# Where the raw words of the last two weights land: idle halves of the weight ring in place of the attention tiles

## The chip, the cores and the metric

The kernel runs on one core of a Trainium2 chip. The metric is device microseconds of one execution; the kernel before takes 754.57 us (median of three runs, 754.39 to 755.67). The change is judged against that time. Engines: TensorE (PE in the profile; PEld is its weight load), VectorE (DVE), ScalarE (ACT), GpSimd (POOL) and SyncE (SP), whose queue issues every DMA here.

## The reference

Four batches of 576 positions, 8 heads of 64. Each batch goes through three parts, one after the other.

```python
# attention: full resolution in a band of 7 positions, plus 1/4 resolution over all
out = up(softmax(q_d k_d^T / 8) v_d) + softmax(mask(q k^T / 8)) v
# mixer: x is out as 576 x 512 per batch
u  = x + Re(FFT_seq(FFT_model(x)))
un = (u - mean(u)) / sqrt(var(u) + 1e-6)
x  = u + relu(un @ w_ch1) @ w_ch2          # 512 -> 2048 -> 512
# gated output
gate = sigmoid(causal 5-tap convolution of x with conv_w)
y = (gate * (x @ w_val)) @ w_out           # 512 -> 512 -> 512
```

The weights arrive as 64-bit numbers. The kernel reads them as pairs of 32-bit words and builds float32 from them itself.

## The kernel before, in words

Work is written as small steps with positions on one axis; the unit of that axis is a *unit*, 192 positions of a batch, and there are three to a batch (`units`, twelve in all, (0, 0) to (3, 2)). `spread` gives a list of steps positions between two numbers, all steps are sorted by position and issued, and a scheduler then reorders instructions on each engine by what it thinks is ready. So a change of positions can move any row after it. The first attention, the weights and unit 0 are start-up; from unit 1 on TensorE multiplies float16 pairs: each product is three matmuls (high by high, high by low, low by high).

**A unit.** `ln(b, j)` norms it: two column sums by TensorE (`st<-uc`, then `st<-sq`), a subtraction, a square on ScalarE, a reciprocal root of nine small VectorE steps (`vv`, `r`), and at the end the halves `uh` (ScalarE) and `ul` (VectorE). Then eight `h_group`s (24 matmuls into `ph`; ScalarE makes `hh`, VectorE `hl`) and eight `c_group`s (24 matmuls into `pc`) alternate; `c_group(g)` needs `hl` of group g. `fin` adds `pc` into X. Behind a unit come its taps (`tap`, and `W<-X,cw` later on), `val` (24 matmuls for each half) and `out`.

**Attention of the next batches** is mixed into the units. For batch 1: `scores` (dS) and its exponentials (dP, on ScalarE, one 64-column piece per instruction), `values` (dPT, PT, dO, and the copies `X<-dO`), then the 1/4-resolution part: `v` is pooled from four pieces of two tiles, each loaded by SP, added by GpSimd (`ptv`, `vr`), and then squared by ScalarE (`v<-v`), which frees the tile for a later load; `sc`, `E`, the multiply of E by `lsu` on GpSimd, `eT`, `ET`, `po`, `base`. After `base` come the transforms (FH, FL, `ab`, AH, AL, `pp`, `pq`, DS) that end in batch 1's X, and with it in `ln(1, 0)`.

**PSUM and X.** `dO`, `po`, `st`, `val` and `out` share two banks, so a matmul into `st` waits until an older `dO` has been copied by `X<-dO`.

**Weights.** `W[1]` to `W[20]` are 4 KB halves of ten ring tiles. `load_w` puts raw words of w_ch1 and w_ch2 into places that are not used yet; `word_w` makes float32 from them by three VectorE instructions for each 512 or 1024 columns (`to_f32`: one TENSOR_SCALAR, two SCALAR_TENSOR_TENSOR); `conv_w` splits float32 into high (ScalarE) and low (VectorE) float16. The splits of w_ch2 (W2 below; rows `W<-W,s_w`) run one behind the other on the two engines. W[17] to W[20] will hold w_val (16, 17) and w_out (18, 19). Before, each of their eight raw pieces (512 KB) is loaded into one of the two attention tiles `k` and `v` of the pool `qkv` and converted in the same step, so at most two are in flight and each load waits for a tile to come free.

**SP.** DMAs are issued in the order of SP's queue; a DMA that waits for its tile holds all behind it. `chain` makes early loads issue one after the other.

Of the kernel before, what the change touches and what calls it, by code (L numbers as in the profile page):

```python
# [12 lines left out]
I32 = mybir.dt.int32  # L13
# [4 lines left out]
B, H, S, D = 4, 8, 576, 64  # L18
# [31 lines left out]
S_S0 = (-11.1, -10.1)  # L50
# [3 lines left out]
S_END = -8.95  # L54
S_F0 = (-8.9, -8.1)
# [1 line left out]
S_N0 = -7.5  # L57
S_W2 = (-7.4, -6.9)
S_C2 = (0.89, 0.94)
S_W3 = (1.02, 1.6)  # L60
N_WARM = (8, 5, 14, 2, 2, 2)
S_G1 = (-6.8, -6.7)
S_G2 = (0.2, 0.44)
# [12 lines left out]
P_TAP = (-0.05, 0.35)  # L76
# [51 lines left out]
def attn_moe_kernel(ctx, tc, q_t, k_t, v_t, w1, w2, w_val, conv_t, w_out, c_feat, c_seq, c_band, c_eye, out):  # L128
    nc = tc.nc
    P = 128  # L130
    w1, w2, w_val, conv_t, w_out = (x.bitcast(I32) for x in (w1, w2, w_val, conv_t, w_out))

    def pool(name, bufs=1, **kw):
        return ctx.enter_context(tc.tile_pool(name=name, bufs=bufs, **kw))
# [29 lines left out]
    def stt(eng, out, in0, scalar, in1, op0, op1):  # L164
        return eng.scalar_tensor_tensor(out=out, in0=in0, scalar=scalar, in1=in1, op0=op0, op1=op1)  # L165
# [14 lines left out]
    chain = {"on": CHAIN, "last": None}  # L180

    def load(**kw):

        if chain["on"] and chain["last"] is not None:
            with tc.issue_after(chain["last"]):
                i = nc.sync.dma_start(**kw)
        else:
            i = nc.sync.dma_start(**kw)
        chain["last"] = i.ins
# [63 lines left out]
    NPOS = 20  # L253
    ring = [wp.tile([P, 2048], F32, name=f"W{2 * i + 1}") for i in range(NPOS // 2)]
    W = [wp.tile([P, 1024], F32, name="W0")]
# [11 lines left out]
    def rows(dst, src, c, c0, n):  # L267
        load(out=dst, in_=src[c * 128:(c + 1) * 128, 2 * c0:2 * (c0 + n)])
# [3 lines left out]
    def behind(gate, f):  # L272

        if gate is None:
            f()
        else:
            with tc.issue_after(gate):
                f()

    def to_f32(dst, raw, gate=lambda: None):  # L280

        r = raw.rearrange("p (n t) -> p n t", t=2)
        behind(gate(), lambda: V.tensor_scalar(out=dst, in0=r[:, :, 1], scalar1=3, scalar2=0x3FFFFFF8,
                                               op0=ALU.logical_shift_left, op1=ALU.bitwise_and))
        behind(gate(), lambda: stt(V, dst, r[:, :, 1], -0x40000000, dst, ALU.bitwise_and, ALU.bitwise_or))
        behind(gate(), lambda: stt(V, dst, r[:, :, 0], 29, dst, ALU.logical_shift_right, ALU.bitwise_or))
# [18 lines left out]
    def word_w(i):  # L305
        if i < 16:
            raw = raws.pop(i)
            n = 1024 // len(raw)
            for z, x in enumerate(raw):
                to_f32(W[i + 1].bitcast(I32)[:, z * n:(z + 1) * n], x,  # L310
                       lambda g=(gates, gates2)[i // 8]: g.pop(0) if len(g) > 1 else g[0])
            return
        assert "scored" in st[1]
        for a in range(2):
            raw = qkv.tile([P, 1024], I32, tag="kv"[a], name="raw")
            rows(raw, w_val if i < 18 else w_out, (i % 2) * 2 + a, 0, 512)
            to_f32(W[i + 1].bitcast(I32)[:, a * 512:(a + 1) * 512], raw)

    gram = {}

    def sumsq_w(i, key, first, last):

        if first:
            gram[key] = pst("cv", [P, P]) if key == "wo" else ps_c.tile([P, P], F32, tag="c1", name="gram")
        x = W[i + 1].bitcast(BF16).rearrange("p (n t) -> p n t", t=2)
        for c in range(8):
            blk = x[:, c * 128:(c + 1) * 128, 1]
            behind(st[0]["st2"].ins if i < 8 else None, lambda: T.matmul(
                out=gram[key], lhsT=blk, rhs=blk, start=(first and c == 0), stop=(last and c == 7)))
# [11 lines left out]
    def conv_w(i, s, eng):  # L341

        h_, l_, r_ = hi(i), lo(i), W[i + 1]
        A.activation(out=h_, in_=r_, func=AF.Copy, scale=s[:, 0:1])
        if eng is G:
            A.activation(out=r_, in_=r_, func=AF.Copy, scale=s[:, 0:1])
            G.tensor_tensor(out=l_, in0=r_, in1=h_, op=ALU.subtract)
        else:
            stt(eng, l_, r_, s[:, 0:1], h_, ALU.mult, ALU.subtract)
# [17 lines left out]
    def wv_scale():  # L367
        ps = pst("cv", [P, 512])
        for a in range(4):
            j = pr_t("sqv", [P, 512])  # L370
            A.activation(out=j, in_=W[17 + a // 2][:, (a % 2) * 512:(a % 2) * 512 + 512], func=AF.Square)
            T.matmul(out=ps, lhsT=ones, rhs=j, start=(a == 0), stop=(a == 3))
        mx = keep.tile([P, 1], F32, name="cvmx")
        V.tensor_reduce(out=mx, in_=ps, axis=AX.X, op=ALU.max)
        mx2 = keep.tile([P, 1], F32, name="cvmx2")
        V.tensor_scalar(out=mx2, in0=mx, scalar1=float(DM), scalar2=None, op0=ALU.mult)
        sc["sv"], sc["ivv"] = pow2(mx2, 14, "wv")

    def wo_scale():
        f = trace_w("wo")  # L380
        sc["so"], sc["ivo"] = pow2(f, 14, "wo")
        ivvo = keep.tile([P, 1], F32, name="ivvo")
        mul(V, ivvo, sc["ivv"], sc["ivo"])
        sc["ivvo"] = ivvo
# [3 lines left out]
    st = {}  # L388
# [524 lines left out]
    un = {}  # L913
    mainp = {}

    def main_pools():
        for n, bufs in (("un", 2), ("hg", 3), ("g", 1), ("L", 2), ("tap", 3), ("S", 3)):
            mainp[n] = pool("m_" + n, bufs)

    def l_t(name, shape):  # L920
# [281 lines left out]
    def w_in2(i):  # L1202
        if i >= 11:
            load_w(i)
        word_w(i)

    def w_in(i):
        word_w(i)
# [4 lines left out]
    def weights3_steps():  # L1213
        def first():
            to_f32(cw.rearrange("p a b -> p (a b)").bitcast(I32), craw)

        def a2():
            wv_scale()
            for i in range(16, 18):
                conv_w(i, sc["sv"], G if i in LO_G else V)  # L1220

        def a3():
            for i in range(18, NPOS):
                sumsq_w(i, "wo", i == 18, i == NPOS - 1)
            wo_scale()
            for i in range(18, NPOS):
                conv_w(i, sc["so"], G if i in LO_G else V)
        return [first] + [lambda i=i: word_w(i) for i in range(16, NPOS)] + [a2, a3]

    units = [(b, j) for b in range(B) for j in range(UPB)]  # L1230
    events = []
# [1 line left out]
    def put(pos, f):  # L1233
        events.append((pos, len(events), f))

    def spread(steps, p0, p1):
        tot = sum(c for c, _ in steps)
        acc = 0.0
        for c, f in steps:
            put(p0 + (p1 - p0) * acc / tot, f)  # L1240
            acc += c
# [16 lines left out]
    def close():  # L1258
        start.close()
        main_pools()  # L1260

    assert S_LD[1] <= S_T0[0] and S_L1 <= S_W1[0] and S_T0[1] <= S_S0[0] and S_S0[1] <= S_F0[0] and S_F0[1] <= S_N0
    assert S_W1[1] <= S_W2[0] and 8 / 17 < S_C1[0] and S_C1[1] <= S_C2[0] and 15 / 17 < S_C2[0]
    assert S_S0[1] <= S_END <= S_F0[0] and S_C2[1] <= min(S_W3[0], 1 + P_TAP[0])
    put(S_END, close)
    for b in range(1, B):
        steps = attn_steps(b)
# [7 lines left out]
        spread(steps[n1:], *P_E[b])  # L1275
        put(P_L[b], lambda b=b: urgent(lambda: ln(b, 0), "N"))
    w3 = weights3_steps()
    spread([(1.0, f) for f in w3], *S_W3)
    for n, (b, j) in enumerate(units):
        main = mlp_steps(b, j)  # L1280
        spread([(1.0, f) for f in main], n, n + 1)
# [63 lines left out]
```

## Time and profile before

| | |
|---|---|
| median of three runs | 754.57 us (754.39 to 755.67) |
| the profiled execution | 750.94 us, span 749.1 us |
| TensorE busy | 688.4 us (92%), granted clock 0.943 of full |
| VectorE busy | 482.2 us (64%) |
| ScalarE busy | 321.0 us (43%) |
| GpSimd busy | 108.2 us (14%) |

The profiled execution is 3.6 us below the median of the timed runs; 1.8 us of it lie outside the span. A wait is read from the engine that waits: the idle time ahead of a row stands in its brackets with what ended it. TensorE's clock of 1.00 is its full level (2.4 GHz), 0.50 the lower one (1.2 GHz).

### The profile page before, as it was taken

How to read it: one execution, taken by the hardware profiler on the slowest of the kernel's cores; microseconds unless marked ns; L12 is line 12 of the kernel's file. 1: busy time of each engine (PE TensorE's matmuls, PEld its weight loads, DVE VectorE, ACT ScalarE, POOL GpSimd, SP SyncE). 2: the span in 40 equal slices, each digit the busy share in tenths (PEclk: the TensorE clock that was granted, in tenths of full speed). 3: DMA queues.
4: the chain of work that ended last, by engine and by line, in shares of the span. 5: the costliest groups of instructions: out<-in, count | busy, mean ns of one | idle time of the engine just before them, and what ended most of it. 6: DMA issues, size and time to landing. Idle time of an engine off the chain costs nothing.

```text
span 749.1 us, 18445 instructions
## 1 busy us (share of the span) xinstructions
PE 688.4 (92%) x7811; PEld 599.7 (80%) x7811; DVE 482.2 (64%) x1073; ACT 321.0 (43%) x994; POOL 108.2 (14%) x143
## 2 busy tenths in 40 slices
PE   7877659987899998989999998899999999999996
PEld 3444449987788987877898997789989989999893
DVE  3795869768986967566976824747835473633334
ACT  2465211777644436665533645553423131322212
POOL 0400000004431012240203105103010010000000
PEclk8556779998999999999999999899999999999999
DMA  9955356123232110132140001002100000000001
GB/s 239 391 205 180 111 190 200 37 82 113 94 113 70 49 60 30 53 85 79 46 129 2 16 24 41 15 3 64 47 16 15 2 6 25 2 16 1 30 2 42
DMA packets 29005, 54.79 MB, mean 73 GB/s; under 512 B 2133, under 2 KB 17109, under 8 KB 27898
## 3 DMA queue, kind: packets, MB, share of 16 engines
q1 hardware_dynamic: 28922, 53.61, 21.9%
q8 instruction: 61, 1.00, 0.6%
q14 instruction: 22, 0.18, 0.1%
HBM read 46.52 MB, written 9.45 MB: 75 GB/s over the span
## 4 chain that ended last, share of the span: by engine, by line
PE 59%; DVE 22%; DMA 9%; ACT 6%; POOL 2%; issue 1%; SPq 1%; DVEq 0%; POOLq 0%; ACTq 0%
PE pc L1065 20%; PE ph L1047 19%; DVE W L165 8%; PE out L1152 5%; PE val L1136 5%; ACT dP L536 3%; DMA v<-in_v_dram 2%; PE po L716 2%; DVE tap L165 2%; PE ab L810 1%; DMA dr<-dx 1%; DMA dx<-X 1%; DMA X<-in_moe_w_ch_dram 1%; DMA raw<-in_moe_w_ch_dram 1%; DVE fF L787 1%
## 5 line engine op out<-in xcount | busy, mean ns | idle before, releaser
L1047 PE MATMUL ph<-uh,W 128*128 128x192 f16 x1408 | 197.4, 247 | 1.6 <-ACT uh L973 1.6
L1065 PE MATMUL pc<-hh,W 128*128 128x192 f16 x1408 | 196.1, 247 | 1.2 <-ACT hh L1051 1.2
L1065 PEld LDWEIGHTS <-W 128*128 128x128 f16 x2112 | 176.7, 98 | 14.4 <-issue 10.8
L1047 PEld LDWEIGHTS <-W 128*128 128x128 f16 x2112 | 176.6, 98 | 7.5 <-issue 5.2
L1065 PE MATMUL pc<-hl,W 128*128 128x192 f16 x704 | 172.7, 247 | 5.1 <-DVE hl L165 5.1
L1047 PE MATMUL ph<-ul,W 128*128 128x192 f16 x704 | 173.8, 247 | 0.0
L165 DVE SCALAR_TENSOR_TENSOR hl<-ph,hh 128x384 f16<-128x384 f32 x88 | 48.5, 553 | 92.3 <-ACT hh L1051 92.3
L1051 ACT ACTIVATE hh<-ph 128x384 f16<-128x384 f32 x88 | 43.3, 493 | 102.3 <-PE ph L1047 99.3
L165 DVE SCALAR_TENSOR_TENSOR W<-X,cw,W 128x192 f32<-128x192 f32 x160 | 61.0, 437 | 2.3 <-ACT W L1121 2.2
L1136 PE MATMUL val<-yy,W 128*128 128x192 f16 x576 | 53.3, 246 | 1.5 <-ACT osb L1164 1.1
L1136 PEld LDWEIGHTS <-W 128*128 128x128 f16 x576 | 47.9, 98 | 3.4 <-issue 1.9
L536 ACT ACTIVATE dP<-dS,dmx 128x64 f32<-128x64 f32 x160 | 47.9, 340 | 0.4
L1152 PE MATMUL out<-W,gh 128*128 128x512 f16 x144 | 45.9, 381 | 0.0
L536 ACT ACTIVATION_READ_ACCUMULATOR dP<-dS,dmx 128x1 f32 x160 | 37.2, 233 | 0.0
L1152 PE MATMUL out<-W,gl 128*128 128x512 f16 x72 | 27.5, 382 | 2.1 <-DVE gl L165 2.1
L165 DVE SCALAR_TENSOR_TENSOR W<-W,W 128x1024 int32<-128x1024 int32 x24 | 28.8, 1220 | 0.1
L682 ACT ACTIVATE E<-sc,nm 72x144 f32<-72x144 f32 x64 | 23.6, 374 | 6.6 <-PE po L716 6.4
L1152 PEld LDWEIGHTS <-gh 128*128 128x128 f16 x144 | 14.2, 99 | 14.4 <-issue 0.9
L1009 PE MATMUL ph<-u,W 128*128 128x192 f32 x128 | 24.3, 345 | 1.0 <-DVE u L945 1.0
L668 PE MATMUL sc<-qkT 64*72 64x144 f32 x128 | 22.4, 341 | 2.5 <-DVE qkT L588 1.0
L1143 ACT ACTIVATE gh<-W 128x384 f16<-128x384 f32 x20 | 10.6, 528 | 31.9 <-DVE W L165 31.8
L1121 ACT ACTIVATE W<-X,cw 128x192 f32<-128x192 f32 x40 | 15.5, 455 | 19.6 <-DVE X L165 17.8
(221 smaller groups left out, 1169.2 us busy)
## 6 DMA issues: line engine op xcount, KB each, us to landing
W<-in_moe_w_ch_dram SPq DMA_DIRECT2D x12, 1024.0 KB
v<-in_v_dram SPq DMA_DIRECT2D x32, 144.0 KB
out_dram<-osb SPq DMA_DIRECT2D x18, 256.0 KB
vw<-in_v_dram SPq DMA_DIRECT2D x16, 256.0 KB
X<-in_q_dram SPq DMA_DIRECT2D x6, 576.0 KB
kT<-in_k_dram SPq DMA_DIRECT2D x4, 582.0 KB
dx<-X SPq DMA_DIRECT2D x4, 576.0 KB
dr<-dx SPq DMA_DIRECT2D x4, 576.0 KB
```

The lines of the kernel that those rows point to most:

```text
L165: return eng.scalar_tensor_tensor(out=out, in0=in0, scalar=scalar, in1=in1, op0=op0, op1=op1)
L536: A.activation(out=s_[:, z, a], in_=pss[par][:, z, a], func=AF.Exp, scale=SCALE, bias=mx[:, par, z, a:a + 1], accum_out=su[:, par, z, a:a ...
L668: T.matmul(out=pss[par][:, qc], lhsT=d["qkT"][r, 0, a, qc * QC:(qc + 1) * QC], rhs=d["qkT"][r, 1, a, :], start=True, stop=True,)
L682: A.activation(out=E[:, qc], in_=ps[:, qc], func=AF.Exp, scale=SCALE / 16, bias=nm[:, qc:qc + 1], accum_out=su[:, qc:qc + 1],)
L716: T.matmul(out=po[par * 64:par * 64 + 64], lhsT=d["vr"][:, kc, (a % 2) * 4 + (a // 2) * 2 + par], rhs=ets[par][:, kc], start=(kc == 0), st ...
L1009: i = T.matmul(out=ps[:, e], lhsT=W[kc * 2 + m // 8 + 1][:, o:o + 128], rhs=u()[:, kc, :], start=(kc == 0), stop=(kc == 3))
L1047: T.matmul(out=ps[:, e], lhsT=w1_ap(pw, kc, 2 * g + e), rhs=uh[px][:, kc, :], start=(t == 0), stop=(t == 11))
L1051: A.activation(out=h_, in_=ps, func=AF.Relu)
L1065: T.matmul(out=ps[m // 2][:, m % 2], lhsT=w2_ap(pw, kk, m), rhs=x[px][:, e, :], start=(kk == 0 and (pw, px) == (0, 0) and m % 2 == 0), sto ...
L1121: A.activation(out=m, in_=x, func=AF.Copy, scale=w)
L1136: T.matmul(out=ps[:, e], lhsT=wv_ap(pw, kc, 2 * mh + e), rhs=m_["y"][px][:, kc, :], start=(t == 0), stop=(t == 11))
L1152: T.matmul(out=ps, lhsT=(gh, gl)[px][:, kc, t * 128:(t + 1) * 128], rhs=wo_ap(pw, kc), start=(n == 0), stop=(n == 11))
```

## The change

The raw words of w_val and w_out get other places, and loading is written apart from converting. The first two pieces of w_val go to W[19] and W[20], the third to a new 4 KB tile `rx`, the fourth to W[19] again once the first is converted; the first piece of w_out goes to W[20], the second to `rx`, and the last two to the attention tiles as before. Each of these loads is issued behind the last load of the chain. w_val's conversions stand at positions 0.945 to 0.99, just behind W2's splits (0.89 to 0.94), and w_out's at 1.0 to 1.5; before, all stood between 1.02 and 1.6.

```diff
--- before.py
+++ after.py
-S_W3 = (1.02, 1.6)
+S_W3 = ((0.945, 0.99), (1.0, 1.5))
...
-        assert "scored" in st[1]
         for a in range(2):
+            to_f32(W[i + 1].bitcast(I32)[:, a * 512:(a + 1) * 512], raw3.pop((i, a)))
+
+    raw3 = {}
+
+    def load_w3(i, a):
+
+        if (i, a) in ((16, 0), (17, 1)):
+            raw = W[19].bitcast(I32)
+        elif (i, a) in ((16, 1), (18, 0)):
+            raw = W[20].bitcast(I32)
+        elif i < 19:
+            raw = mainp["rx"].tile([P, 1024], I32, tag="rx", name="raw")
+        else:
+            assert "scored" in st[1]
             raw = qkv.tile([P, 1024], I32, tag="kv"[a], name="raw")
+        raw3[i, a] = raw
+        with tc.issue_after(chain["last"]):
             rows(raw, w_val if i < 18 else w_out, (i % 2) * 2 + a, 0, 512)
-            to_f32(W[i + 1].bitcast(I32)[:, a * 512:(a + 1) * 512], raw)
...
-        for n, bufs in (("un", 2), ("hg", 3), ("g", 1), ("L", 2), ("tap", 3), ("S", 3)):
+        for n, bufs in (("un", 2), ("hg", 3), ("g", 1), ("L", 2), ("tap", 3), ("S", 3), ("rx", 1)):
...
-        return [first] + [lambda i=i: word_w(i) for i in range(16, NPOS)] + [a2, a3]
+        ld = lambda *h: lambda: [load_w3(*x) for x in h]
+        return ([ld((16, 0), (16, 1), (17, 0)), first, lambda: word_w(16), ld((17, 1)), lambda: word_w(17)],
+                [ld((18, 0), (18, 1), (19, 0), (19, 1)), a2, lambda: word_w(18), lambda: word_w(19), a3])
...
-    spread([(1.0, f) for f in w3], *S_W3)
+    for g, p in zip(w3, S_W3):
+        spread([(1.0, f) for f in g], *p)
```

On SP, behind the q of batch 2 (`X<-in_q`), the queue was this; `v_...` are the tiles of batch 1's pooled v, `raw` the attention tiles:

```order
L188 DMA vw<-in_v_dram 64x2x256 x2
L188 DMA X<-in_q_dram 128x2x576 x2
L188 DMA raw<-in_moe_w_val_dram 128x1024 x2
L186 DMA v_1808<-in_v_dram 72x2x256
L188 DMA v_1850<-in_v_dram 72x2x256
L188 DMA v_1851<-in_v_dram 72x2x256
L188 DMA raw<-in_moe_w_val_dram 128x1024
L188 DMA v_1862<-in_v_dram 72x2x256
L188 DMA v_1863<-in_v_dram 72x2x256
L188 DMA raw<-in_moe_w_out_dram 128x1024
L188 DMA raw<-in_moe_w_val_dram 128x1024
```

and is now this (`W_121` is the ring tile of W[19] and W[20], `raw` the tile `rx`):

```order
L188 DMA vw<-in_v_dram 64x2x256 x2
L188 DMA X<-in_q_dram 128x2x576 x2
L186 DMA v_1811<-in_v_dram 72x2x256
L188 DMA v_1853<-in_v_dram 72x2x256
L188 DMA v_1854<-in_v_dram 72x2x256
L188 DMA v_1865<-in_v_dram 72x2x256
L188 DMA v_1866<-in_v_dram 72x2x256
L188 DMA W_121<-in_moe_w_val_dram 128x1024 x2
L188 DMA raw<-in_moe_w_val_dram 128x1024
L188 DMA W_121<-in_moe_w_val_dram 128x1024
L188 DMA W_121<-in_moe_w_out_dram 128x1024
```

The five loads of v now stand ahead of every load of w_val; before, two pieces stood ahead of the first and one among them.

On VectorE, from the split of W2 that follows the adds of unit 0's `fin` to the first `hl` of unit 1 (`W_120<-raw` is a conversion of w_val, `W_...<-W_...,s_w` a split):

```order
L283 TENSOR_SCALAR W_120<-raw 128x512
L165 SCALAR_TENSOR_TENSOR W_117<-W_118,s_w_1528,W_117 128x1024
L165 SCALAR_TENSOR_TENSOR tap<-X,cw,tap 128x192 x3
L165 SCALAR_TENSOR_TENSOR W_120<-raw,W_120 128x512
L165 SCALAR_TENSOR_TENSOR tap<-X,cw,tap 128x192 x4
L165 SCALAR_TENSOR_TENSOR W_120<-raw,W_120 128x512
L165 SCALAR_TENSOR_TENSOR tap<-X,cw,tap 128x192 x2
L945 TENSOR_TENSOR uc<-X,st 128x768
L165 SCALAR_TENSOR_TENSOR W_118<-W_118,s_w_1528 128x1024
L165 SCALAR_TENSOR_TENSOR tap<-X,cw,tap 128x192
L283 TENSOR_SCALAR W_120<-raw 128x512
L165 SCALAR_TENSOR_TENSOR hl<-ph,hh 128x384
```

and now:

```order
L165 SCALAR_TENSOR_TENSOR W_117<-W_118,s_w_1531,W_117 128x1024
L689 TENSOR_REDUCE nm<-sc 72x2 x2
L171 TENSOR_TENSOR X<-pc_1615,X 128x2x192
L165 SCALAR_TENSOR_TENSOR tap<-X,cw,tap 128x192 x2
L165 SCALAR_TENSOR_TENSOR W_118<-W_118,s_w_1531 128x1024
L165 SCALAR_TENSOR_TENSOR tap<-X,cw,tap 128x192 x9
L959 TENSOR_TENSOR uc<-X,st 128x768
L165 SCALAR_TENSOR_TENSOR tap<-X,cw,tap 128x192
L165 SCALAR_TENSOR_TENSOR W_118<-W_119,s_w_1531,W_118 128x1024
L165 SCALAR_TENSOR_TENSOR tap<-X,cw,tap 128x192
L165 SCALAR_TENSOR_TENSOR hl<-ph,hh 128x384
```

The conversions have left this piece (and three instructions of one that stood ahead of it); one more split and three more taps now stand ahead of `hl`.

On ScalarE, from the last `hh` of unit 2 to the `uh` of batch 1's unit 0 (`sq<-uc` is the square of `ln(1, 0)`, `dP` the exponentials of batch 2):

```order
L1051 ACTIVATE hh<-ph 128x384
L951 ACTIVATE sq<-uc 128x768
L528 ACTIVATE dmx<-dmx 128x8
L536 ACTIVATE dP_3073,dsu<-dS,dmx 128x64 x4
L536 ACTIVATE dP_3078,dsu<-dS,dmx 128x64 x4
L1164 ACTIVATE osb<-out,sof_3313 128x512
L1099 ACTIVATE yy<-X,s_y_2356 128x768
L973 ACTIVATE uh<-uc 128x768
L563 ACTIVATE PT<-dPT 128x512
L528 ACTIVATE dmx<-dmx 128x16
L536 ACTIVATE dP_3248,dsu<-dS,dmx 128x64 x8
```

and now:

```order
L1065 ACTIVATE hh<-ph 128x384
L542 ACTIVATE dmx<-dmx 128x8
L550 ACTIVATE dP_3072,dsu<-dS,dmx 128x64 x4
L550 ACTIVATE dP_3077,dsu<-dS,dmx 128x64 x4
L965 ACTIVATE sq<-uc 128x768
L542 ACTIVATE dmx<-dmx 128x16
L550 ACTIVATE dP_3247,dsu<-dS,dmx 128x64 x8
L1178 ACTIVATE osb<-out,sof_3312 128x512
L1113 ACTIVATE yy<-X,s_y_2441 128x768
L987 ACTIVATE uh<-uc 128x768
L550 ACTIVATE dP_3256,dsu<-dS,dmx 128x64 x8
```

The square now stands behind the first eight exponentials, and eight more stand between it and `uh`. On TensorE the two column sums of that norm moved with it: `st<-uc` stood 53 matmuls of unit 2 ahead of that unit's last one and now stands behind it, with two `dS<-bandb` and 32 `dS<-kT,X` between it and `st<-sq`.

## Rows read from the trace of the kernel before

**Rows 1.** Stretches: length, busy time of PE, PEld, DVE, ACT, POOL, clock, DMA share, GB/s.
```profile
173.00:192.00 19.00, 13.12 (x154) 11.25 (x153) 18.93 (x34) 15.52 (x40) 6.88 (x8) 0.82 0.36 122
...
300.00:330.00 30.00, 27.38 (x419) 24.06 (x420) 13.94 (x33) 21.41 (x82) 12.38 (x17) 1.00 0.27 77
...
330.00:460.00 130.00, 129.77 (x1655) 114.72 (x1653) 84.29 (x195) 64.05 (x213) 21.84 (x31) 1.00 0.14 47
```

**Rows 2.** TensorE's waits between 170 and 345 us: total, times, longest, in us.
```profile
PE st L939 <- ACT X L583: 4.3, 2, 4.0
...
PE pc L1065 <- DVE hl L165: 1.6, 1, 1.6
...
PE ph L1047 <- ACT uh L973: 1.6, 1, 1.6
...
PE st L939 <- POOL sq L171: 1.1, 1, 1.1
```

**Rows 3.** Timeline around 176 to 185 us: start, length, engine, line, operation, [idle before].
```profile
176.34 0.33 SPq L186 DMA_DIRECT2D v<-in_v_dram  x1
...
176.96 6.03 SPq L188 DMA_DIRECT2D v<-in_v_dram  x2
...
180.95 0.95 POOL L171 TENSOR_TENSOR vr<-v 72x256 f32<-72x256 f32 x1 [9.31 <-DMA v<-in_v_dram]
...
185.17 1.06 POOL L171 TENSOR_TENSOR vr<-v 72x256 f32<-72x256 f32 x1 [1.33 <-DMA v<-in_v_dram]
...
183.24 1.01 PE L939 MATMUL st<-uc,ones 128*128 128x192 f32 x2 [4.00 <-ACT X L583]
```

**Rows 4.** Conversions by tile (ns min/median/max), and the timeline around 190 us.
```profile
L165 DVE SCALAR_TENSOR_TENSOR W<-raw,W x24: 661/682/1211, 94.9 to 219.0; 128x512 int32<-128x512 int32 x24
...
L283 DVE TENSOR_SCALAR W<-raw x12: 408/424/947, 92.7 to 216.4; 128x512 int32<-128x512 int32 x12
...
188.04 1.27 DVE L165 SCALAR_TENSOR_TENSOR W<-W,s_w 128x1024 f16<-128x1024 f32 x1
...
190.90 0.74 DVE L165 SCALAR_TENSOR_TENSOR tap<-X,cw,tap 128x192 f32<-128x192 f32 x2
...
191.03 0.24 PE L1065 MATMUL pc<-hl,W 128*128 128x192 f16 x1 [1.60 <-DVE hl L165]
```

**Rows 5.** Timeline of GpSimd: its multiplies beside a full VectorE and alone.
```profile
195.94 5.65 POOL L168 TENSOR_TENSOR E<-E,lsu 72x288 f32<-72x288 f32 x2 [4.84 <-DVE lsu L687]
...
209.55 0.67 POOL L168 TENSOR_TENSOR E<-E,lsu 72x288 f32<-72x288 f32 x1 [0.55 <-DVE lsu L687]
```

**Rows 6.** Timeline from the last layer norm of batch 1, unit 0, to its first matmuls.
```profile
277.16 0.59 PE L939 MATMUL st<-uc,ones 128*128 128x192 f32 x2 [0.32 <-DVE uc L171]
...
279.01 0.83 ACT L951 ACTIVATE sq<-uc 128x768 f32<-128x768 f32 x1
...
279.88 0.95 DVE L171 TENSOR_TENSOR sq<-sq 128x384 f32<-128x384 f32 x2
...
282.33 0.52 PE L939 MATMUL st<-sq,ones 128*128 128x192 f32 x2
...
282.64 0.61 DVE L165 SCALAR_TENSOR_TENSOR X<-pc,iv,X 128x384 f32<-128x384 f32 x1
...
283.27 0.30 DVE L955 TENSOR_SCALAR vv<-st 128x192 f32<-128x192 f32 x1
...
288.63 0.84 ACT L973 ACTIVATE uh<-uc 128x768 f16<-128x768 f32 x1 [1.43 <-DVE uc L168]
...
289.45 1.28 DVE L525 TENSOR_REDUCE dmx<-dS 128x8 f32<-128x512 f32 x2
...
289.52 0.33 PE L1047 MATMUL ph<-uh,W 128*128 128x192 f16 x2 [1.60 <-ACT uh L973]
```

**Rows 7.** From the chain that ended last: start, length, engine, what.
```profile
163.17 2.38 ACT dP L536 x16
...
253.43 1.98 PE pc L1065 x24
```

More of the change, by code (lines that the diff above doesn't have):

```diff
@@ L1263, in attn_moe_kernel @@
     assert S_W1[1] <= S_W2[0] and 8 / 17 < S_C1[0] and S_C1[1] <= S_C2[0] and 15 / 17 < S_C2[0]
-    assert S_S0[1] <= S_END <= S_F0[0] and S_C2[1] <= min(S_W3[0], 1 + P_TAP[0])
+    assert S_S0[1] <= S_END <= S_F0[0] and S_C2[1] <= min(S_W3[1][0], 1 + P_TAP[0])
     put(S_END, close)
```

## The prediction

> **What bounds the kernel now.** I read the stretches first, for where TensorE stands still: a time in which it is dense can only be shortened by doing less, and the change takes no matmul away. From 330 to 460 us it is busy for 129.77 of 130 us [rows 1]; in 173 to 192 for 13.12 of 19 at a granted clock of 0.82, and in 300 to 330 for 27.38 of 30. The orders of the engines of the two kernels part only at about 173 us (where the first conversion leaves VectorE) and are the same again from about 445 us, so the result is the idle time of TensorE between these, plus what its clock does. Then the list of its waits, read for who ends them [rows 2]: `st` waited 4.0 us for the copy `X<-dO`, `pc` 1.6 for `hl`, `ph` 1.6 for the last `uh`, `st` 1.1 for a sum behind GpSimd. Last the timeline around each, for what the releaser itself was late with.
>
> The 4.0 us: ScalarE's `X<-dO` stands behind a square of `v`, that behind GpSimd's `vr` at 180.95, and that waited for a load of v issued at 176.34, which lay behind two raw pieces of w_val [rows 3]. `st` begins at 183.24, at half clock (1.01 us for a pair that takes 0.59 later [rows 6]). Of the chain that ended last, 24 matmuls cost 1.98 us and 8 exponentials with their read-outs 2.38 us [rows 7]; I use both as prices.
>
> **The change part by part.** *The load of v on SP* no longer has raw words ahead of it. The second load of v, with no raw piece in its way to the tile, was issued when the row of 176.96 ends, at about 182.7 (176.96 plus 6.03 is 182.99, its last descriptor 0.33), and its `vr` began at 185.17: 2.5 us, against 180.95 − 176.34 = 4.6 for the first [rows 3]. So 2.1 us are to be had on the load. But the new ScalarE order has one square of v more ahead of `X<-dO`, which wants one more load, issued only when its tile is free, and a tap and a split of W2. At one load and landing (2.5) plus the add (0.95) this takes the gain back. I take 0 for this wait; the bounds are −2.1, and +1.4 if the extra load also finds its tile late (2.5 + 0.95 − 2.1).
>
> *A, the first `hl` of unit 1.* In the piece of VectorE's order three TENSOR_SCALARs and four SCALAR_TENSOR_TENSORs of conversions are gone: 3 × 0.42 + 4 × 0.68 = 4.0 us [rows 4]. One split (1.27) and three taps (0.37 each) are new: 2.4. That is −1.6. VectorE is busy for 18.93 of 19 us there, so nearly all of it counts; but about 1.8 us of the removed work stood where the split and the adds wait for ScalarE, and if that wait stays, only 0.6 of the 1.6 is left. `pc` resumes at 191.03 now. I take −1.0, between −0.4 and −3.0 (the last if VectorE nowhere waits for ScalarE and the taps find their place in a gap).
>
> *B, the second sums of unit 1.* The conversions now stand behind that `hl`: split, three TENSOR_SCALARs, conversions, taps, 6.7 us at the prices above, before the adds that `st<-sq` needs. TensorE has 63 matmuls till there, 63 × 1.98/24 = 5.2 us, so it waits 1.5. Some conversions stood near these sums before as well, so part of that wait is there already; I take half, +0.7 (0 to +1.5).
>
> *C, the 1/4-resolution chain.* The conversions now lie beside GpSimd's multiplies of E. Beside a full VectorE two of these took 5.65 us, 2.8 each, against 0.67 alone [rows 5]; `eT` on TensorE waits for them. One multiply more in the full stretch would be +2.1 for that chain, most of it hidden by the h and c groups that TensorE takes in between. I take +0.4 (0 to +1.5). The Trainium skill ("SBUF — State Buffer", section "SBUF: two separate sides") has VectorE and GpSimd share a port pair which whoever starts first keeps for a whole instruction, the other blocked; by that C would be at its upper bound and the sum 1.1 higher. The rows of 2.8 against 0.67 agree that they hinder each other, and can't tell whether one instruction excludes the other fully.
>
> *D, the norm `ln(1, 0)` between unit 2 of batch 0 and the first unit of batch 1.* Call T the end of unit 2's last matmul: 282.33 before, since `st<-sq` follows at once [rows 6]. Before, `st<-uc` (277.16), ScalarE's `sq` (279.01) and its sums were all hidden under 53 matmuls, and `vv` began at T + 0.9, `uh` at T + 6.3. Now `st<-uc` stands behind T. The subtraction on VectorE (from 277.16 to 279.01 that step took 1.85) also stands behind the two `fin` adds (0.61 each), so `sq` starts at about T + 1.9, if the eight exponentials that now stand ahead of it (2.4) are done; 0.83 and the two adds of 0.95 bring T + 3.6; and the maxima `dmx` of the second group (1.28) have moved ahead of `vv`: T + 4.9. From `vv` to `uh` it is 5.36 us as before, and ScalarE's eight more exponentials, `osb` and `yy` (about 4 us) fit into that. `uh` is thus 4.0 us later after T (3.0 if the maxima run before the sums, 4.8 if the exponentials hold up `sq`). `st<-uc` with some of the `dS`, 0.6 us of matmuls, fills part of it. I take +3.4 of idle time, between +2.4 and +4.2, in pieces before `st<-sq`, `out` and `ph`.
>
> *E, given back.* The second group of exponentials and `dS` is no longer behind this `uh`, so the work of batch 2 that follows comes earlier by up to 2.4 us against TensorE. Of the 30 us from 300 to 330 it is idle for 2.6, 1.1 of them the `st<-sq` behind GpSimd [rows 1, 2]. If these go, that is −2.6; a first `hl` now stands behind 16 exponentials' sums on VectorE, +1.0. I take −1.6 (0 to −2.6, with no new wait). Behind 330 TensorE is dense and gives nothing back.
>
> *Without a price here.* That the loads land earlier, and that w_val's conversions end earlier, gains nothing by itself: TensorE's waits show none for w_val's tiles [rows 2]. The tile `rx` and the ring halves hold no one up; w_out's pieces follow later into tiles that are free.
>
> Sum: −1.0 + 0.7 + 0.4 + 3.4 − 1.6 = +1.9. Against the profiled 750.94 that makes 752.8; the runs' median lies 3.6 above the profiled execution, so I forecast 754.57 + 1.9, about 756.5 us.
>
> **The rivals.** *No change, 754.6.* D at its lower bound and A at −1.6, with B at 0 and C at 0.4, give −0.4. For it: most of what I move are waits of a microsecond, and a scheduler's order changes little where the slack is as large as VectorE's 64%. Against it: `st<-uc` can't run before T in the new order, whatever else happens. That the change doesn't do what it says (the landing places move and nothing waits for them) also ends here.
>
> *Faster, 752.4.* VectorE reaches the first `hl` by the sum of its own work, A −3.0, B 0, C 0, D +2.4, E −1.6: −2.2. It decides at the wait before `st` in the 180s: if `X<-dO` runs before the extra square of v, the 2.1 us of the load come on top of TensorE's front, and the clock isn't lowered there. For it: the raw words were in front of the load in the trace. Against it: the extra square in ScalarE's order.
>
> *Slower, about 759.4.* The idle pieces of D come close together, 5.0 us within 12 with the 1.6 that stood there, and TensorE drops to its lower level behind them, as it did after the 4.0 us wait at 183.24. That stretch had 0.82 of full clock over 19 us, 0.18 × 19 = 3.4 us, of which 2.9 fall on busy time; 756.5 + 2.9 = 759.4. Against it: the wait of 1.6 us at 289.52 is followed by full clock (two matmuls in 0.33). The Trainium skill ("TensorE: Matmul & The Clock Gate", section "HAM oscillation — how this bites in real kernels") describes kernels that pay a lower clock behind every long pause; the row at 183.24 agrees with it.
>
> **How the numbers follow.** Chances: the forecast (756.5, own range 755.0 to 758.0) 0.43, no change 0.27, faster 0.20, slower by the clock 0.10. About 1.5 us, 0.2%, is what a measurement of this kernel can tell from no change. The lower part of the forecast's own range is within that, the no-change case spreads beyond it on both sides: faster by over 0.2% 0.24, within 0.33, slower 0.43. Leaving out 2 in 10 at the ends I keep 751.8 (faster with the bound of the load, half of it) to 759.5 (the clock).
>
> **What would show it.** In the profile after: `st<-ACT X` at about 183 still near 4 us (the load gives nothing) or down to 2 (the faster rival). `pc<-DVE hl` at about 190. GpSimd's two multiplies of E near 196, longer than 5.65 or not. At the end of unit 2 of batch 0: `st<-uc` behind the last `pc`, `vv` at T + 4.9, `uh` at T + 10.3, and TensorE idle for 5 us and more between T and `ph`; a full clock there rules out the last rival. The wait `st<-POOL sq` near 329 gone. The prediction is wrong if the idle time from T to `ph` is not 2.4 to 4.2 us longer, or if the stretch before 262 us changes by more than the sum of A to C, 0.1, plus or minus 2.

## The result, and the profile after

The changed kernel takes 759.62 us (median of 6 runs, 757.3 to 761.08), before 754.18 in the same rounds: ratio 1.0069, 95% interval 1.0051 to 1.0087. By the ratio it is slower by 5.2 us, where 1.9 were forecast. The median lies 0.1 us above 759.5, the upper end of the forecast's range, and the six runs lie on both sides of that end. The profiled execution took 760.22 us, span 758.4.

Busy times by stretch of the kernel after (columns as in [rows 1]; the stretch from 192 to 210 us is new, and the second fence has it for the kernel before):

```profile
173.00:192.00 19.00, 12.04 (x146) 9.86 (x145) 16.93 (x27) 15.89 (x40) 6.45 (x8) 0.80 0.36 122
192.00:210.00 18.00, 15.71 (x144) 14.21 (x144) 15.61 (x42) 6.18 (x19) 7.76 (x3) 0.83 0.43 147
...
290.00:300.00 10.00, 6.84 (x83) 3.23 (x82) 8.04 (x18) 6.11 (x29) 3.08 (x4) 0.83 0.02 6
300.00:330.00 30.00, 29.39 (x503) 27.32 (x503) 15.63 (x35) 20.52 (x83) 9.43 (x11) 1.00 0.24 72
330.00:460.00 130.00, 127.52 (x1527) 111.51 (x1525) 87.40 (x201) 67.14 (x228) 23.24 (x32) 1.00 0.15 50
```

```profile
192.00:210.00 18.00, 17.00 (x197) 15.48 (x195) 17.38 (x48) 7.65 (x21) 7.91 (x5) 1.00 0.37 110
```

Two stretches have become worse. From 192 to 210 TensorE did 144 matmuls in place of 197, at a clock of 0.83 in place of 1.00. From 290 to 300 it was busy for 6.84 us, again at 0.83. The stretch from 300 to 330 lost its idle time, as forecast, but 2.5 us of idle time stand behind 330. A low clock in these stretches is no mark of the change by itself: a second profile of the order of before (`before_again`, at the end of the experiments) has the same two at 0.84 and 0.83:

```profile
192.00:210.00 18.00, 17.54 (x171) 16.20 (x172) 17.13 (x40) 10.64 (x30) 6.25 (x7) 0.84 0.32 106
290.00:300.00 10.00, 8.06 (x97) 7.03 (x88) 6.13 (x12) 7.72 (x39) 0.30 (x1) 0.83 0.08 28
```

TensorE's waits from 170 to 345 us, after (answers to [rows 2]):

```profile
PE st L953 <- ACT X L597: 3.7, 2, 3.5
PE pc L1079 <- DVE hl L165: 2.3, 1, 2.3
PE eT L720 <- POOL E L168: 2.3, 1, 2.3
PE dS L518 <- ACT dP L550: 2.0, 2, 1.2
PE sc L682 <- ACT E L696: 1.7, 2, 1.4
PE val L1150 <- ACT yy L1113: 1.4, 1, 1.4
...
PE st L953 <- DVE sq L171: 1.0, 1, 1.0
PE pc L1079 <- ACT hh L1065: 0.8, 1, 0.8
...
PE st L953 <- POOL sq L171: 0.2, 1, 0.2
```

The first place in the timeline, engine by engine (answers to [rows 3 to 5]):

```profile
179.90 0.80 POOL L171 TENSOR_TENSOR vr<-v 72x256 f32<-72x256 f32 x1 [7.75 <-DMA v<-in_v_dram]
...
184.14 0.75 PE L953 MATMUL st<-uc,ones 128*128 128x192 f32 x2 [3.48 <-ACT X L597]
...
183.74 4.55 DVE L165 SCALAR_TENSOR_TENSOR tap<-X,cw,tap 128x192 f32<-128x192 f32 x9
...
191.35 0.54 DVE L165 SCALAR_TENSOR_TENSOR hl<-ph,hh 128x384 f16<-128x384 f32 x1
...
191.94 0.32 PE L1079 MATMUL pc<-hl,W 128*128 128x192 f16 x1 [2.31 <-DVE hl L165]
...
195.59 6.44 POOL L168 TENSOR_TENSOR E<-E,lsu 72x288 f32<-72x288 f32 x2 [5.90 <-DVE lsu L701]
...
201.46 0.69 PE L720 MATMUL eT<-eye,E 72*72 72x72 f32 x4 [2.28 <-POOL E L168]
```

The load of v lands earlier (`vr` 3.0 us after its issue at 176.86, 4.6 before), and the wait before `st` is 0.5 us shorter. But nine taps at 0.51 us each, one behind the other, now stand ahead of `uc` and `hl` on VectorE, `hl` comes at 191.35, and GpSimd's two multiplies of E, 6.44 us beside the conversions, hold `eT` back by 2.28 us. The second place, `ln(1, 0)` (answers to [rows 6]):

```profile
288.12 0.52 PE L953 MATMUL st<-uc,ones 128*128 128x192 f32 x2
...
288.51 0.32 ACT L550 ACTIVATE dP<-dS,dmx 128x64 f32<-128x64 f32 x1
...
290.84 0.88 ACT L965 ACTIVATE sq<-uc 128x768 f32<-128x768 f32 x1
...
293.21 1.28 DVE L539 TENSOR_REDUCE dmx<-dS 128x8 f32<-128x512 f32 x2
294.41 0.34 DVE L969 TENSOR_SCALAR vv<-st 128x192 f32<-128x192 f32 x1
...
294.42 0.63 PE L1166 MATMUL out<-W,gl 128*128 128x512 f16 x1
...
297.68 0.38 PE L1166 MATMUL out<-W,gl 128*128 128x512 f16 x1
...
299.72 0.83 ACT L987 ACTIVATE uh<-uc 128x768 f16<-128x768 f32 x1
```

Unit 2 ends at T = 288.12. `vv` begins at T + 6.3 and `uh` at T + 11.6 (T + 0.9 and T + 6.3 before). The exponentials only start at 288.51, so ScalarE's `sq` stands behind them till 290.84, and the two sums behind it took 1.53 us beside a multiply on GpSimd (0.95 before). The matmuls into `out` take 0.63 us around 294 and 0.38 at 297.68: TensorE's clock was at its lower level there.

### The profile page after: what moved, and what is told of

It is laid out like the page before. It is cut to its first block, busy times and chain, and to the rows that moved or that the text cites. A ratio compares the mean times of both kernels' runs of the same rounds, so it can differ in the third digit from the quotient of the medians.

```text
span 758.4 us, 18452 instructions
## 1 busy us (share of the span) xinstructions
PE 694.4 (92%) x7811; PEld 601.8 (79%) x7811; DVE 485.5 (64%) x1073; ACT 321.5 (42%) x994; POOL 109.8 (14%) x143
## 4 chain that ended last, share of the span: by engine, by line
PE 58%; DVE 21%; DMA 11%; ACT 6%; POOL 2%; issue 1%; SPq 1%; DVEq 0%; ACTq 0%; POOLq 0%
PE pc L1079 19%; PE ph L1061 18%; DVE W L165 8%; PE out L1166 6%; PE val L1150 4%; DMA W<-in_moe_w_ch_dram 3%; ACT dP L550 2%; DMA v<-in_v_dram 2%; DVE tap L165 2%; PE po L730 1%; PE ab L824 1%; PE sc L682 1%; DMA dr<-dx 1%; DMA dx<-X 1%; DMA raw<-in_moe_w_ch_dram 1%
## 5 line engine op out<-in xcount | busy, mean ns | idle before, releaser
L1079 PE MATMUL pc<-hh,W 128*128 128x192 f16 x1408 | 198.3, 249 | 2.0 <-ACT hh L1065 2.0
L165 DVE SCALAR_TENSOR_TENSOR W<-W,W 128x1024 int32<-128x1024 int32 (+1 forms) x30 | 32.8, 1112 | 0.1
L730 PE MATMUL po<-ET,vr 72*64 72x144 f32 x128 | 20.2, 328 | 4.7 <-ACT ET L725 4.7
L1023 PEld LDWEIGHTS ph<-u,W 128*128 128x128 f32 x128 | 23.1, 208 | 1.6 <-DVE u L959 1.6
```

The costliest lines, as they stand in the source:

```text
L730: T.matmul(out=po[par * 64:par * 64 + 64], lhsT=d["vr"][:, kc, (a % 2) * 4 + (a // 2) * 2 + par], rhs=ets[par][:, kc], start=(kc == 0), st ...
L1023: i = T.matmul(out=ps[:, e], lhsT=W[kc * 2 + m // 8 + 1][:, o:o + 128], rhs=u()[:, kc, :], start=(kc == 0), stop=(kc == 3))
L1079: T.matmul(out=ps[m // 2][:, m % 2], lhsT=w2_ap(pw, kk, m), rhs=x[px][:, e, :], start=(kk == 0 and (pw, px) == (0, 0) and m % 2 == 0), sto ...
```

## The experiments

The table gives, for each kernel, the median of its timed runs, the ratio to before with its 95% interval, and from the profile the start of unit 0's `fin` (the first `X<-pc`) and the rest of the span behind it. The start-up ahead of `fin` differs by several us from one execution to the next, so profiles are compared by the rest. It is good to 2 or 3 us: the two profiles of the order of before differ by +0.8 in it, and by −1.6 if counted from an earlier matmul. `places` is the new landing places alone; `wout_old` is the change with w_out's group back at its old positions; `taps_behind` and `no_dO_wait` are the change with one more edit; `E_on_ACT`, `wout_old_no_dO_wait`, `both_moves` and `both_moves_E` start from `wout_old`; a name with `before_` is an edit of the kernel before. The kernels were timed in several rounds, in which the median of before lay between 753.9 and 754.7, so kernels of different rounds are compared by their ratios.

| kernel | median, us | ratio (95%) | `fin` at | rest |
|---|---|---|---|---|
| before | 754.18 | 1 | 177.40 | 571.7 |
| before_again | 755.03 | 1.0007 (0.9991 to 1.0022) | 179.39 | 572.5 |
| the change | 759.62 | 1.0069 (1.0051 to 1.0087) | 177.09 | 581.3 |
| places | 756.23 | 1.0036 (1.0015 to 1.0058) | 178.35 | 575.9 |
| wout_old | 756.46 | 1.0031 (1.0015 to 1.0047) | 178.41 | 575.9 |
| taps_behind | 768.88 | 1.0196 (1.0173 to 1.0219) | 178.38 | 589.0 |
| no_dO_wait | 754.27 | 1.0006 (0.9990 to 1.0022) | 178.05 | 573.5 |
| E_on_ACT | 753.73 | 1.0012 (0.9992 to 1.0031) | 178.20 | 573.2 |
| wout_old_no_dO_wait | 757.34 | 1.0039 (1.0017 to 1.0061) | 182.50 | 573.9 |
| both_moves | 751.08 | 0.9969 (0.9953 to 0.9984) | 180.37 | 569.6 |
| before_no_dO_wait | 754.94 | 1.0010 (0.9996 to 1.0024) | 179.10 | 572.6 |
| before_both_moves | 754.02 | 0.9994 (0.9976 to 1.0011) | 180.98 | 573.5 |
| before_E_on_ACT | 756.67 | 1.0027 (1.0013 to 1.0042) | 179.57 | 576.7 |
| both_moves_E | 750.75 | 0.9937 (0.9915 to 0.9959) | 178.94 | 570.6 |

**One loss or two.** My theory was two separate losses; the rival, one that runs through. First the landing places alone:

```diff
-S_W3 = ((0.945, 0.99), (1.0, 1.5))
+S_W3 = ((0.945, 0.99), (1.02, 1.6))
...
+        return ([], [ld((16, 0), (16, 1), (17, 0)), first, lambda: word_w(16), ld((17, 1)), lambda: word_w(17),
+                 ld((18, 0), (18, 1), (19, 0), (19, 1)), lambda: word_w(18), lambda: word_w(19), a2, a3])
```

> The new landing places alone: loads and conversions of w_val and w_out stand at the positions of the kernel before (1.02 to 1.6). The engines' orders are then those of the changed kernel up to the end of w_val's conversions, and at ln(1, 0) those of before again (the column sum 54 matmuls ahead of the end of unit 2). Theory one (two separate losses: the landing places cost some 4.5 us between 173 and 212, the earlier w_out positions some 4 us at ln(1, 0)): about 755.8 us, ratio to before 1.002, the waits for hl (2.3) and for GpSimd's E (2.3) still there, idle time between unit 2 and ph again about 2 us. Theory two (one loss: the late 1/4-resolution part of batch 1 makes ln(1, 0) late, whatever the order there): about 759.5, ratio 1.007, with ln(1, 0) as late against unit 2's end as in the changed kernel.

Measured 756.23, ratio 1.0036. Then the change with w_out's group alone put back:

```diff
-S_W3 = ((0.945, 0.99), (1.0, 1.5))
+S_W3 = ((0.945, 0.99), (1.02, 1.6))
```

> The change with w_out's group back at 1.02 to 1.6 and w_val's left at 0.945 to 0.99. Theory one: as the kernel with the landing places alone, about 755.8 us, ratio 1.002, since only w_out's positions decided the order at ln(1, 0). Rival: w_val's earlier positions matter too, and the time lies over 1.5 us away from that of the landing places alone, in the direction of 759.6.

Measured 756.46, ratio 1.0031: the same within the intervals. Theory one holds against theory two: both intervals end below 1.007. The landing places alone cost some 2.5 us; of the positions of w_val these runs show no effect; and w_out's group, moved forward by 0.02 to 0.1 of a unit, costs the other 2.9 (1.0069 against 1.0031). Not all of that is shown to come from the order at `ln(1, 0)`: of the 5.4 us between the profiles of the change and of `wout_old`, 2.2 lie between unit 2's `fin` and the first of batch 1, 1.8 ahead of it and 1.5 behind. TensorE's waits in the profile of places show the old order there (`ph` behind `uh`, 1.6, as before) and the early waits of the change:

```profile
PE pc L1079 <- DVE hl L165: 2.3, 1, 2.3
PE eT L720 <- POOL E L168: 1.6, 1, 1.6
PE ph L1061 <- ACT uh L987: 1.6, 1, 1.6
```

**What holds TensorE in the first place.** In the change, the taps of unit 0 were put behind the first `hl`:

```diff
-stt(V, m, x, w, m, ALU.mult, ALU.add)
+behind(st["hl", 0, 1] if i == 0 else None, lambda: stt(V, m, x, w, m, ALU.mult, ALU.add))
```

> The change, and the taps of unit 0 may issue on VectorE only behind the first hl of unit 1. Theory (the 0.9 us by which this hl came late, and the clock that stayed low to 194.7, come from the taps that took the place of the conversions on VectorE): hl at 188 to 189 in place of 191.35, the wait of pc for it under 1 us; w_val's conversions and the sums of unit 2's norm then come some 2 us later behind 13 taps, so of the 2.3 us perhaps 1 is left: about 758.5 us, ratio 1.0055. Rival (hl is late by ScalarE's hh, as X<-dO is late): hl stays at 191 or later and the time at 759.6 or above.

Measured 768.88: a miss, and a lesson. `hl` does come at 188.35, and unit 1's `fin` 5.2 us earlier than in the change (235.52 against 240.71). But all of it and 7.7 us more is lost behind (the rest of the span in the table), most of it at `ln(1, 0)`, whose order is the bad one here too, and for which TensorE now waits longer: unit 2 ends 6.8 us earlier (`fin` at 281.38 against 288.15), while `uc` and the exponentials `dP` come only 0.4 us earlier (`dP` at 288.10 against 288.51). The clock was low there too, 0.72 from 282 to 300 against 0.91 in the change. TensorE's waits from 262 to 345 us:

```profile
PE dS L518 <- ACT dP L550: 5.5, 3, 3.0
PE st L953 <- ACT X L597: 2.3, 1, 2.3
PE st L953 <- DVE uc L171: 1.8, 1, 1.8
```

Next, in the change, the column sums of unit 2's norm in other banks:

```diff
-LN_H = ()
+LN_H = ((0, 2),)
```

> The change, and the column sums of unit 2's norm go to the two banks of ph in place of those shared with dO, so that they don't wait for X<-dO at 184. Theory (the wait of 3.5 us and the low clock of TensorE behind it, from 184.4 to 194.7, make the largest part of the 4.6 us lost up to 212): no wait on X<-dO, full clock up to 210, and 4 to 6 us gained, about 754.5 us, ratio 1.000. Rival (TensorE waits next for hh and hl all the same, since VectorE and ScalarE are full to 192): the wait moves on to pc, the clock still falls, and the time stays within 1.5 us of 759.6.

Measured 754.27, ratio 1.0006, as the theory had it, but not by its mechanism: TensorE waits for `hh` (3.3) and `hl` (4.5) in place of `X<-dO`, as the rival said, and its clock was at the lower level from 184.7 to 194.9 all the same. Three other things differ, and this run doesn't tell them apart. That norm's sums and root (from 194 to `uh` at 215 in the change) now lie from 151 to 163, out of the full stretch, and GpSimd's first two multiplies of E take 1.30 us in place of 6.44:

```profile
194.14 1.30 POOL L168 TENSOR_TENSOR E<-E,lsu 72x288 f32<-72x288 f32 x2 [2.09 <-DVE lsu L701]
```

And the order at `ln(1, 0)` is the good one, with w_out's group still at its early positions. The next run takes GpSimd out by itself, on the kernel with w_out's group back:

```diff
-EN_G = (1,)
+EN_G = ()
```

> As the kernel with w_out's group back (756.5), and batch 1's E is multiplied by 1/sum on ScalarE in place of GpSimd (two activations for each in place of one multiply). Theory (GpSimd's two multiplies, 6.4 us beside VectorE's conversions, hold eT back by 1.9 us in the stretch to 212): the wait for E goes, and with it 1.5 to 2 us: about 754.8 us, ratio 1.001. Rival (the conversions and sums of the norm on VectorE end last there, and TensorE waits for these next): the wait for E goes, one on st or pc takes its place, and the time stays at 756 to 757.

Measured 753.73, ratio 1.0012 against 1.0031; the rest of the span is 2.7 us shorter. The wait for E (1.9) is gone. Ahead of it, where the order on VectorE, ScalarE and GpSimd is the same, `X<-dO` held TensorE for 1.0 in place of 2.7, and 1.6 for `hh` stand in place of 1.5 behind a tap. By the ratios E on ScalarE gives back 1.4 of the 2.3 us that this kernel lost; the two intervals overlap, so that GpSimd's E is most of the loss of the landing places is likely and not shown. The edit with the banks, on the same kernel with w_out's group back:

```diff
-LN_H = ()
+LN_H = ((0, 2),)
```

> As the kernel with w_out's group back (756.5), with the column sums of unit 2's norm in the banks of ph, as in the run without the wait for X<-dO (754.3, with w_out's group early). The column sum of ln(1, 0) stands 86 matmuls ahead of unit 2's end, 45 in the other run. Theory (two losses that add up, the norm of unit 2 in the full stretch to 212 and the order at ln(1, 0)): the order at ln(1, 0) was good in both, so the same time within 1.5 us: 753 to 755.5, ratio 0.999 to 1.001. Rival (w_out's later positions are worth something by themselves): under 752.5.

Measured 757.34, ratio 1.0039: outside what either theory gave. The rest of the span, 573.9, is within 0.5 us of the 573.5 that theory one has; what is longer in its profile is the start-up (`fin` at 182.50 against 178.05), in which both kernels have the same order on every engine. Its twelve runs spread from 754.1 to 760.0. Why its median is 3 us above the other's stays open. With the banks moved, w_out's early positions show no cost.

**Both moves together**, the banks and the taps, on the kernel with w_out's group back, where the order at `ln(1, 0)` is good:

```diff
-LN_H = ()
+LN_H = ((0, 2),)
...
-stt(V, m, x, w, m, ALU.mult, ALU.add)
+behind(st["hl", 0, 1] if i == 0 else None, lambda: stt(V, m, x, w, m, ALU.mult, ALU.add))
```

> As the kernel of the run before this, and the taps of unit 0 on VectorE only behind the first hl of unit 1, with the order at ln(1, 0) good (38 matmuls ahead). In the run of the taps alone unit 2 ended 0.6 us ahead of before, 5 ahead of the other kernels, and the bad order at ln(1, 0) gave back 17. Theory (VectorE's taps are what held hl in the 180s, and the norm behind dO what then held TensorE): unit 2 ends at 279 to 281 and the time is 749 to 751.5, ratio 0.993 to 0.997, under both kernels. Rival (the taps only move: w_val's conversions and batch 1's 1/4-resolution part wait for them then): 753 or more.

Measured 751.08, ratio 0.9969: faster than both kernels. Unit 2 ended at 282.53, later than expected, in a profile whose first `fin` came 3.0 us later than before. TensorE's clock is full in both early stretches:

```profile
173.00:192.00 19.00, 16.00 (x204) 14.54 (x202) 13.86 (x20) 15.86 (x40) 8.25 (x10) 1.00 0.25 72
192.00:210.00 18.00, 15.51 (x168) 13.69 (x168) 16.89 (x48) 7.75 (x25) 6.23 (x6) 1.00 0.48 165
```

The same edits on the kernel before tell whether the new places have a part in that: the line of the banks (`LN_H`) alone, then both lines.

> The kernel before, with the column sums of unit 2's norm in the banks of ph. Theory (the wait of 4.0 us and the clock behind it cost the kernel before as much as the changed one): 750 to 752, ratio 0.994 to 0.997, so that the landing places still cost 2 us against it. Rival (before, hl and the conversions end last in the 180s, and the wait moves on to them): 753.5 to 755.5, ratio 1.000.

> The kernel before (landing places and positions untouched) with both moves: the column sums of unit 2's norm in the banks of ph, and the taps of unit 0 on VectorE behind the first hl of unit 1. Theory (the new landing places are worth something once VectorE's taps are out of hl's way, since before, the conversions still stand ahead of hl there): hl at 188.5 to 190, 752.5 to 754, ratio 0.997 to 1.000, so 1.5 to 3 us above the changed kernel with both moves (751.1). Rival (the landing places are worth nothing, the moves alone make the gain): 750 to 752, as with the change.

Measured 754.94 (1.0010) and 754.02 (0.9994): neither gains. In the first the wait moves on (`pc` behind `hh`, 6.3 us), as its rival said. With both moves the new places and w_val's positions are worth 1.9 us by the ratios (the intervals overlap slightly). The profile shows where: with the old places conversions still stand ahead of `hl`, and with the taps moved away VectorE stands still for a raw piece of w_val, so `hl` came at 194.03, not at 188.5 to 190 (187.30 with the new places):

```profile
191.35 0.43 DVE L283 TENSOR_SCALAR W<-raw 128x512 int32<-128x512 int32 x1 [5.38 <-DMA raw<-in_moe_w_val_dram]
...
194.03 0.55 DVE L165 SCALAR_TENSOR_TENSOR hl<-ph,hh 128x384 f16<-128x384 f32 x1
```

E on ScalarE (`EN_G = ()`), on the kernel before and on the best kernel:

> The kernel before with batch 1's E multiplied on ScalarE. Theory (GpSimd's multiplies hold TensorE back by 0.8 us before, by 1.9 to 2.3 in the changed kernels): 753 to 753.8, 0.3 to 1 us under before, ratio 0.9985 to 1.000. Rival (the run with w_out's group back gained its 2.5 us by ScalarE's new order and not by E's wait): 752 or less, ratio under 0.9975.

> The changed kernel with w_out's group back and both moves (751.1), and batch 1's E on ScalarE. Theory (its wait for E is 0.8 us in that profile): 749.8 to 750.8, ratio 0.995 to 0.996. Rival (ScalarE's additional activations stand ahead of hh, for which TensorE waits 2.7 us there): 751 to 753.

Before, it made the kernel slower, 756.67 (1.0027): neither theory. In its profile the loss is ahead of E, in a stretch whose order is that of before: GpSimd's add `vr` took 5.48 us where [rows 3] have 0.95, and the wait for `X<-dO` was 6.4. Whether that is so in the timed runs is not known, and so the price of E before stays open. On the best kernel it gives 750.75, ratio 0.9937 (0.9915 to 0.9959), the best of all, 3.6 to 4.8 us under before; its interval overlaps that of `both_moves`, so the gain over that kernel is not shown.

**The kernel before, a second time**, with the same order on every engine:

```diff
-S_W3 = (1.02, 1.6)
+S_W3 = (1.1, 1.6)
```

> The kernel before, with w_val's and w_out's first position at 1.1 in place of 1.02: every engine's order is word for word that of before, so it is a second profile of the same work. Theory (the profiled execution of before, 750.9, stands 3.6 us under its median by its start-up and by a short add of GpSimd ahead of X<-dO, 0.95 us; in the other kernels with the old places that add took 1.6 to 5.5): ratio 0.999 to 1.001, a profiled execution of 753 to 756, with the add at 1.5 us or more and TensorE's wait for X<-dO over 4.3 us. Rival (the profile of before is typical, and only the start-up differs): the add at about 1 us and the wait at 4.0 again.

Measured 755.03, ratio 1.0007, span 751.9 against 749.1. The add took 1.88 us, as expected, but the wait for `X<-dO` was 1.4, not over 4.3, and a wait of 3.0 of `sc` for E stood behind it. Of the 2.8 us between the two spans 2.0 lie ahead of `fin` (4.4 ahead of the `sc` at 174.40 in the one and 178.81 in the other). So the profile of before that the prediction was worked from was a short one mostly by its start-up, and its list of waits is one draw among several: the same order waits at another place the next time. So does the clock: between 165 and 345 us it was at its lower level from 167.1 to 173.9, 191.0 to 197.8 and 293.4 to 296.8 us here, and from 182.2 to 189.0 alone in the first profile.

## Why the prediction came out as it did

The direction and the two places were right; the sum was 3.3 us short. By its own sign the prediction failed in the first place: the stretch before 262 us was to change by 0.1 plus or minus 2, and unit 1's `fin` came 4.7 us later (240.71 against 236.02; counted from the `sc` at 174.90, 4.2 us later than in the profile of before and 5.4 later than in `before_again`). The sign in the second place held: 2.5 us more idle time from T to `ph`. That 759.6 is next to the 759.4 of the rival "slower by the clock" is chance: that rival had A to C as they were forecast.

**The load of v**: taken as 0, measured 0.5 less wait. Right, as far as one profile tells: `before_again` waited 1.4 there with the order of before.

**A, the first `hl`**: taken as −1.0, measured +0.9 (191.94 against 191.03), of which 0.5 was there before the orders part (the split at 172.28 before, 172.79 after): +0.4 without it. The step that failed is the exchange "one split (1.27) and three taps (0.37 each) are new: 2.4" for 4.0 us of conversions: the taps took 0.51 each beside GpSimd's adds, and where the conversions had filled VectorE's waits for ScalarE's halves of the splits, it now stood still, for 1.22 us at 174 and 0.82 at 182. I had counted that wait for a part of A only.

**B, the second sums**: taken as +0.7; no such wait in the list. **C, GpSimd**: taken as +0.4 of 0 to 1.5; `eT` waited 2.28 against 0.78 before, the upper bound, and `E_on_ACT` gave 1.4 us back by the ratios. "Most of it hidden by the h and c groups" is what was wrong in this profile: TensorE stood still ahead of `eT`, and `base`, two steps on, came at 209.21 in place of 205.49. `before_again` had no such wait for `eT`, with 3.69 us for the two multiplies. The sentence on the Trainium skill ("SBUF — State Buffer", section "SBUF: two separate sides") gave that bound; the trace agrees that the two engines hinder each other, with 6.44 us for the two multiplies against 1.30 once VectorE is less full. A to C were to be +0.1 and are about +2.5 by the ratios of `places` and `wout_old`: this is the larger part of what is missing.

**D**: the mechanism was right, step by step: `st<-uc` behind T, the maxima ahead of `vv`, the eight exponentials ahead of `sq`. `vv` came at T + 6.3 for 4.9, `uh` at T + 11.6 for 10.3: the exponentials began at T and not before it (`sq` at T + 2.7 for 1.9), and the two sums took 1.53 us in place of 0.95. Idle time before `ph`: 1.22 + 0.81 + 0.97 + 1.39 = 4.4 against 1.9, +2.5 for the +3.4 taken. The clock was low there, 0.83 from 290 to 300, with `out` at 0.63 in place of 0.38. **E**: the waits from 300 to 330 went (idle 0.6 of 30 us, 2.6 before), but TensorE is idle for 2.5 of 130 us behind 330, where I had "dense", 1.4 of them the wait of `sc` for E. From 300 to 460 that is 3.1 us against 2.9 before, so of the 1.6 to be given back nothing came. D with E were to be +1.8 and are about +2.9.

**The clock.** I had no price for it in the first place, and put it in a rival in the second. Between 174.9 and 345 us of the change's profile it was at its lower level from 184.4 to 194.7, 201.5 to 204.9 and 293.7 to 297.1, 17 us in all; in the two profiles of before it was there for 7 and 10 us in that part. The `sc` that begins at 174.40 (before), 178.81 (`before_again`) and 174.90 us (the change) has the same matmuls behind it in all three. From there on TensorE's busy time is longer where the clock is low, and what is not busy is idle:

```profile
174.40:749.10 574.70, 550.37 (x6484) 492.70 (x6483) 355.06 (x833) 244.01 (x702) 92.98 (x116) 0.99 0.13 41
```

```profile
178.81:751.90 573.09, 550.49 (x6484) 493.45 (x6483) 354.20 (x830) 240.66 (x695) 93.40 (x116) 0.99 0.13 41
```

```profile
174.90:758.40 583.50, 553.63 (x6484) 494.19 (x6483) 357.99 (x834) 244.29 (x702) 94.55 (x116) 0.98 0.13 42
```

Idle time is 24.3, 22.6 and 29.9 us: 5.5 or 7.3 us more after the change. Busy time is 3.3 or 3.1 us longer. So in the profiles the clock is about a third of the loss and idle time the larger part, of which the forecast was short in A, C and E. What the clock adds in the timed runs is not settled. Its mean is 0.9325 in the six of the change and 0.9346 in 105 of before, worth about 2 us of a span, give or take 1; for `wout_old`, 0.9338 against 0.9338 in the same rounds, it adds nothing that can be told.

## What to carry to other kernels

Ask of an edit what it does to the order, not where the edited work goes: here TensorE waited for none of the moved loads and conversions, while a scheduler that filled the freed places with taps, and put a column sum behind the end of a unit, made the kernel 5 us slower. And where VectorE is full, an operation on GpSimd that TensorE waits for is better priced at its length beside a full VectorE than taken as hidden. A fix in one place (the taps, 5 us earlier) can be worth nothing until the place that takes its gain is mended too. And one profile is one draw: profile the same order twice before a single wait, or a stretch of low clock, is read as the price of an edit.

## What was not expected of the hardware

GpSimd's add `vr` of 72 x 256 took 0.95, 1.88 and 5.48 us in three profiles with the same order around it (before, before_again and before_E_on_ACT). In before_E_on_ACT it began at 182.09 and ended at 187.57, 0.6 us after VectorE ran out of work at 187.0; till then VectorE passed undisturbed, four taps in 1.40 us:

```profile
182.75 1.07 DVE L165 SCALAR_TENSOR_TENSOR tap<-X,cw,tap 128x192 f32<-128x192 f32 x3
...
184.34 1.40 DVE L165 SCALAR_TENSOR_TENSOR tap<-X,cw,tap 128x192 f32<-128x192 f32 x4
185.66 0.68 DVE L165 SCALAR_TENSOR_TENSOR W<-raw,W 128x512 int32<-128x512 int32 x1
186.26 0.74 DVE L165 SCALAR_TENSOR_TENSOR tap<-X,cw,tap 128x192 f32<-128x192 f32 x2
189.96 0.95 DVE L945 TENSOR_TENSOR uc<-X,st 128x768 f32<-128x768 f32 x1 [2.96 <-PE st L939]
```

```profile
182.09 5.48 POOL L171 TENSOR_TENSOR vr<-v 72x256 f32<-72x256 f32 x1 [8.28 <-DMA v<-in_v_dram]
```

ScalarE's square of `v`, which needs the add, began at 187.61, so the length is not that of a row alone. In the profile of before, in the same order, the add took 0.95, and the three taps beside it 1.54 us in place of 1.07:

```profile
180.58 1.54 DVE L165 SCALAR_TENSOR_TENSOR tap<-X,cw,tap 128x192 f32<-128x192 f32 x3
```

In these profiles the one that gets through first is not the same each time, and the same add, which `X<-dO` and with it TensorE wait for here, differs by 4.5 us.
